# FNet and feed-forward on one core: sums of the second layer's moving side one by one among the remainders, other places for weights' sums

## The chip, the core and the metric

The kernel runs on one core of a Trainium2 chip. A core has a matrix engine, TensorE (PE), and three engines for elementwise work: VectorE (DVE), ScalarE (ACT) and GpSimd (POOL). SyncE (SP) issues most of the DMA transfers. The metric is device time of one launch in microseconds (us). The kernel before takes 688.23 us, the median of 3 runs (687.84 to 688.51). The profile is of one further execution of 686.36 us.

## The reference

One sequence of 2048 rows with 512 columns, and a feed-forward layer of 1792 columns, all in fp32:

```python
a = jnp.einsum("bsd,ed->bse", x, dft_hid_re)
b = jnp.einsum("bsd,ed->bse", x, dft_hid_im)
y = jnp.einsum("ts,bse->bte", dft_seq_re, a) - jnp.einsum("ts,bse->bte", dft_seq_im, b)
...
h = x + A_ref(layernorm(x), dft_seq_re, dft_seq_im, dft_hid_re, dft_hid_im)
h2 = h + B_ref(layernorm(h), w1, w2)     # B_ref(x) = silu(x @ w1) @ w2
```

## The kernel before, in words

**Three matmuls for one.** PE multiplies in fp32r, which holds fewer bits than fp32. Each fp32 operand is split into a rounded part (hi) and a remainder (lo). ACT writes the rounded part (L147) and DVE subtracts it from the source to get the remainder (L151). A product is then three matmuls, hi by hi, hi by lo, lo by hi (L196 to L198). In the names, `ph`, `gth` are rounded parts and `pl`, `gtl` their remainders. A remainder waits for its rounding, and a matmul that reads it waits for the remainder.

**Seven products for eight.** The sequence transform and both feed-forward layers use a scheme with seven products of blocks in place of eight. It needs sums and differences of the blocks ahead of the products, on both sides, and sums of the products behind them. For the second layer's moving side (the activations `g`) these are four subtractions for each pair `p` of blocks, in the function `sums_g` (L900). They are done in place: the first two make the operands of products 5 and 7, the last two those of products 6 and 4. Products 1, 2 and 3 read the blocks as they are or rounded before.

**The stages on the core.** `plain(0,0)` to 94 us, `fast(1,0)` to 168, `mix(0)` to 213, `fast(0,1)` and `fast(1,1)` to 367, `mix(1)` to 411: the transform along the sequence, and along the columns. Then the feed-forward layer: `up(0)` to 482 us, `down(0)` with its first products (1, 2 and 3) to about 507 and the others (6, 7, 5 and 4) to 546, `up(1)` to 614, `down(1)` likewise to 680. `norm_h(q, tau)` normalises the rows of half `q` between them: a mean (`m`), centring (`hr`), a square, a variance (`v`), a root, a scaling and a store to `nd`. Its two sums over all partitions are done by POOL (L624).

**What sets the order.** The program is a list of events, each with a planned time. `at(t, f)` puts one at a time, and `step(n, f, before, after)` puts `n` matmuls at the running clock of PE, with other events that stand a given number of microseconds ahead or behind. The sorted list sets the order of instructions on each of PE, DVE, ACT and POOL. Nothing overtakes on these engines: an instruction that waits holds those behind it. Planned times are only a means to sort; the instructions run as soon as what they wait for is done. SP's transfers are in program order too, and a load into a page waits for the page's last readers.

**Places.** There are 51 pages in SBUF, given out by a planner that follows the same planned times, so another time for an event also gives other pages to what comes after. PSUM has 4 tiles of 2 banks. `bank[n]` collects product `n` of the second layer over all seven pairs. When the last pair is done, ACT copies the bank to a page, `keep_bank(n)` (L918, `p` in the names), and the bank's place is used by another product. DVE's adds at L914 then put the kept products together into `r`.

**Numbers named below.** `LEADS` and the times in the loop over `sums_x` set when sums, roundings and remainders of `plain` and `fast` stand ahead of their products. `NORM_US` has the planned starts of `norm_h`, counted from the end of `mix(q)`. `sums_w1` and `make_w2` prepare the weights.

Of the kernel before, what the change touches and what calls it, by code (L numbers as in the profile page):

```python
# [12 lines left out]
ALU = mybir.AluOpType  # L13
# [16 lines left out]
WARM = 13  # L30
MM_US = 0.2265
PREP_US = 8.0
LEADS = (((0, 16.5, 6, 5), (1, 11, 6, 1), 10.5, 8.5),
         ((0, 21, 9, 6), (1, 16, 9, 7), 15, 13))
LOAD_US = 18.0
FETCH_US = 13.0
NORM_US = (-2, 62), (5, 6)
GAP_US = 2.2
FREE_US = {None: 2.0, "matmul": 4.0, "dma_start": 10.0}
ORDERED = (mybir.EngineType.PE, mybir.EngineType.DVE, mybir.EngineType.Activation, mybir.EngineType.Pool)  # L40

# [87 lines left out]
def program(nc, page, keep, small, psum, dram, x, xT, seq, hid, ffn, out):  # L129
# [27 lines left out]
    def halves(lead, make):  # L157

        kept = []
        return [(lead + GAP_US, lambda: kept.append(make())), (lead, lambda: kept.pop()())]  # L160

# [38 lines left out]
    events, clock = [], [0.0]  # L200
# [11 lines left out]
    def at(t, f):  # L212
        events.append((t, 1, len(events), f))
# [41 lines left out]
    def norm_x(jj, which, factors, direct=False, done=False):  # L255

        for k in sorted({k for k, _ in which}):
            if (jj, k) not in xc:
                xc[jj, k] = page(f"xc{jj}{k}")
            for i in range(2):  # L260
                if (i, k, jj) not in X:
                    X[i, k, jj] = page(f"X{i}{k}{jj}", F32R, (2, 2, 256))

        def put(o, k, a, e):
            bias, scale = factors[k, a]
            nc.scalar.activation(o, xraw[jj, k][:, a, e], AF.Identity, bias=bias, scale=scale)

        todo = []
        for k, a in which if direct else ():
            for i in range(0 if done else 2):  # L270
                put(X[i, k, jj][:, 0, a], k, a, slice(i * 256, (i + 1) * 256))
            put(xc[jj, k][:, a, :], k, a, slice(0, 512))
            todo += [(X[i, k, jj][:, 1, a], xc[jj, k][:, a, i * 256 : (i + 1) * 256], X[i, k, jj][:, 0, a]) for i in range(2)]
        if not direct:
            for k, a in which:
                put(xc[jj, k][:, a, :], k, a, slice(0, 512))
        for k in sorted({k for k, _ in which}):
            tiles = [a for kk, a in which if kk == k]
            b = slice(tiles[0], tiles[-1] + 1)
            if tiles[-1] == 1:  # L280
                xraw.pop((jj, k))
            for i in range(0 if direct else 2):
                t, src = X[i, k, jj], xc[jj, k][:, b, i * 256 : (i + 1) * 256]
                nc.scalar.activation(t[:, 0, b], src, AF.Copy)
                todo.append((t[:, 1, b], src, t[:, 0, b]))
        return todo

    def rest(todo):
        for o, a, b in todo:
            nc.vector.tensor_tensor(o, a, b, op=ALU.subtract)  # L290
# [13 lines left out]
    def round_s(jj, sums):  # L304
        todo = []
        for n, v in enumerate(sums):
            t = X["S", n + 1, jj] = page(f"S{n + 1}{jj}", F32R, (2, 2, 256))
            nc.scalar.activation(t[:, 0], v, AF.Copy)
            todo.append((t[:, 1], v, t[:, 0]))
        return todo  # L310

    late = {}

    def early(key, f):
        late[key] = f()
# [60 lines left out]
    def plain(c, q):  # L376
# [47 lines left out]
        for a in range(2):  # L424
            step(24, lambda a=a: [mul(0, 0, tau, [a], part[key]) for tau, key in enumerate(keys)])
        at(-98.5, lambda: load_x(0, 1))
        at(2.4, lambda: early("x0", lambda: norm_x(0, [(1, 0), (1, 1)], late.pop("r0")(), True)))
        at(6.4, lambda: rest(late.pop("x0")))
        for jj, k, tau in [(jj, k, tau) for jj in range(NJ) for k in range(2) for tau in range(2)][2:]:
            key = ("A", c, q, jj, k, tau)  # L430
            before = [(LOAD_US, lambda jj=jj, k=k, tau=tau, key=key: load_seq(c, q, jj, k, tau, key)),
# [1 line left out]
            after = []  # L433
# [17 lines left out]
                after.append((0, evac))  # L451
                after += [(4, lambda i=i, tau=tau: store_c(q, i, tau)) for i in range(2)]
            step(24, lambda jj=jj, k=k, tau=tau, key=key: mul(jj, k, tau, (0, 1), part.pop(key)), before, after)
        for jj, t in enumerate((32, 54, 76, 81)):
            at(t, lambda jj=jj: early(("s", jj), lambda: sums_x(jj)))
            at(t + 3, lambda jj=jj: early(("s", jj), lambda: round_s(jj, late["s", jj])))
            at(t + 6, lambda jj=jj: rest(late.pop(("s", jj))))

    def fast(c, q):

# [411 lines left out]
    def down(q, later):  # L872
# [17 lines left out]
        def round_two(p, f, names):  # L890
            (hi, lo), remainder = rounded(g[q, f], "gt")
            for tau, n in enumerate(names):
                mov[n, p] = hi[:, tau, :], lo[:, tau, :]
            return remainder

        def sums_g(p):
            a, b = g[q, 2 * p], g[q, 2 * p + 1]
            b11, b12, b21, b22 = a[:, 0, :], a[:, 1, :], b[:, 0, :], b[:, 1, :]
            for x, y, z in ((b11, b12, b11), (b12, b22, b12), (b22, b22, b11), (b21, b21, b22)):
                nc.vector.tensor_tensor(x, y, z, op=ALU.subtract)  # L900

        def mul(n, p, ms=(0, 1)):
            if p == 0 and 0 in ms:
# [12 lines left out]
        def keep_bank(n):  # L916
            kept[n] = page(f"p{n}")
            nc.scalar.activation(kept[n], bank[n], AF.Copy)  # L918
# [43 lines left out]
        for p, ns in [(0, (1, 2)), (1, (1, 2)), (0, (3,)), (1, (3,))] + [(p, ns) for p in range(2, NP) for ns in ((1, 2), (3,))]:  # L962
            before, after = [], []
            if ns == (1, 2):
                before = [(FETCH_US, lambda p=p: fetch_w2(p, U, 0)), *halves(PREP_US + 1, lambda p=p: round_one(p)),
                          *halves(PREP_US, lambda p=p: round_two(p, 2 * p + 1, (2, 3)))]
                if p == NP - 2 and not later:
                    before += [(LOAD_US, lambda k=k: load_r(*k)) for k in ((0, 0), (0, 1))]
            if p == NP - 1:
                after = [(0, lambda n=n: keep_bank(n)) for n in ns]  # L970
            step(6 * len(ns), lambda p=p, ns=ns: [mul(n, p) for n in ns], before, after)
            if (p, ns) == (0, (1, 2)):
                yield
        if not later:
            for n, f in enumerate((lambda: add(kept[2], kept[2], kept[1]), lambda: add(r[0, 0], r[0, 0], kept[2]),
                                   lambda: store(0, 0), lambda: add(r[0, 1], r[0, 1], kept[3]))):
                at(clock[0] + 19 + n, f)
        first = clock[0] - PREP_US - 9
        for p in range(NP):
            t = first + 5 * p  # L980
            at(t - 2 * GAP_US - 1, lambda p=p: sums_g(p))
            for d, f in (*halves(1, lambda p=p: round_two(p, 2 * p, (5, 7))),
                         *halves(0, lambda p=p: round_two(p, 2 * p + 1, (4, 6)))):
                at(t - d, f)
        whole, part4 = (0, 1), (0, 1) if later else (0,)
        order = [(n, p, part4 if n == 4 else whole) for p in range(4) for n in (6, 7, 5, 4)]
        order += [(n, p, part4 if n == 4 else whole) for n in (6, 7, 5, 4) for p in range(4, NP)]
# [12 lines left out]
            sums_later(clock[0] + 8)  # L1000

    plain(0, 0)
    for p, t in enumerate((16, -52, -35, 27, 79, 81, 13)):
        sums_w1(clock[0] + t, p)
    fast(1, 0)
    mix(0)
    fast(0, 1)
    fast(1, 1)
    mix(1)
    for p, t in enumerate((-341, -367, -21, -9, -31, 30, 43)):  # L1010
        make_w2(clock[0] + t, p)
    second = down(0, True), down(1, False)
    up(0, 57, lambda: next(second[0]))
    list(second[0])
    up(1, 24, lambda: next(second[1]))
    list(second[1])

    nc.vector.memset(warm, 0.0)
# [45 lines left out]
```

## Time and profile before

| | before |
|---|---|
| median of 3 runs | 688.23 us (687.84 to 688.51) |
| profiled execution | 686.36 us |
| its span | 684.4 us |
| granted clock of PE | 1.00 |
| PE busy | 676.9 us (99%), 2965 matmuls |
| DVE busy | 555.7 us (81%) |
| ACT busy | 338.8 us (50%) |
| POOL busy | 79.9 us (12%) |

The span is the part of the execution that the profiler sees, from the first instruction to the last. "L196 PE MATMUL f<-gth,wf" is a matmul of line 196 that reads `gth` and `wf` and writes `f`, and "<-ACT p L918" behind it says that the idle time before it ended when ACT had written `p` at line 918. In a timeline the first column is the start in us, the second the length of one or of several that follow each other (x3).

### The profile page before, as it was taken

Reading aid. Unit: us, or ns where it says so; the run is one execution under the profiler, and the core shown is the slowest. Engines: PE = TensorE matmul, PEld = TensorE weight load, DVE = VectorE, ACT = ScalarE, POOL = GpSimd, SP = SyncE. Lnnn points to the kernel's source line nnn. Section 1 sums busy time; section 2 is a strip of 40 time slices with the busy share of each in tenths; the row PEclk is TensorE's granted clock in tenths of the full one; section 3 lists DMA queues with packets and bytes.
Section 4 is the critical chain, followed back from the end, with each engine's and each line's share of the span. In section 5 each row is a group of like instructions: output and inputs, shape, how many; then the busy total and the mean of one; then the engine's idle time right before and its main releaser. Section 6 shows DMA issues by size and latency. Waiting matters only on the chain.

```text
span 684.4 us, 8367 instructions
## 1 busy us (share of the span) xinstructions
PE 676.9 (99%) x2965; PEld 554.7 (81%) x2965; DVE 555.7 (81%) x713; ACT 338.8 (50%) x422; POOL 79.9 (12%) x103
## 2 busy tenths in 40 slices
PE   8999999999999999999999999999999999999997
PEld 5888888888888888878888888888878888888785
DVE  6699997996938798996998998877999545549984
ACT  4754775444333443533453544657654444565510
POOL 1012110100103200230000115521000000000000
PEclk9999999999999999999999999999999999999999
DMA  8845889875387667567884699569996566466802
GB/s 319 326 152 233 275 315 369 299 263 185 129 305 276 212 187 278 205 246 278 303 340 162 227 415 332 177 240 339 418 368 230 200 273 239 181 249 252 296 37 92
DMA packets 57289, 174.90 MB, mean 256 GB/s; under 512 B 6432, under 2 KB 13856, under 8 KB 57248
## 3 DMA queue, kind: packets, MB, share of 16 engines
q1 hardware_dynamic: 46896, 138.56, 56.6%
q0 software_dynamic: 10208, 35.68, 13.7%
q8 instruction: 23, 0.38, 0.2%
q14 instruction: 18, 0.15, 0.1%
q10 hardware_dynamic: 144, 0.13, 0.1%
HBM read 135.54 MB, written 38.81 MB: 255 GB/s over the span
## 4 chain that ended last, share of the span: by engine, by line
PE 45%; DVE 10%; issue 1%; ACT 0%; DVEq 0%; ACTq 0%
PE y L196 6%; PE y L198 6%; PE y L197 6%; DVE gtl L151 4%; PE f L196 3%; PE f L197 3%; PE f L198 3%; PE m L197 3%; PE m L198 3%; PE m L196 3%; DVE g L900 3%; PE vx L196 3%; PE vx L198 3%; PE vx L197 3%; DVE pl L151 1%
## 5 line engine op out<-in xcount | busy, mean ns | idle before, releaser
L147 ACT ACTIVATE ph<-raw 128x1024 fp32r<-128x1024 f32 x98 | 101.5, 1057 | 106.1 <-DVE raw L508 62.9
L151 DVE TENSOR_TENSOR pl<-raw,ph 128x1024 fp32r<-128x1024 f32 x98 | 124.3, 1281 | 18.1 <-ACT ph L147 18.0
L197 PE MATMUL m<-pl,S 128*128 128x512 f32 x192 | 74.9, 390 | 0.2 <-DVE pl L151 0.2
L198 PE MATMUL m<-ph,S 128*128 128x512 f32 x192 | 74.7, 389 | 0.0
L196 PE MATMUL m<-ph,S 128*128 128x512 f32 x192 | 74.7, 389 | 0.0
L783 DVE TENSOR_TENSOR g<-vx,g 128x512 f32<-128x512 f32 x42 | 28.9, 688 | 48.7 <-PE vx L198 19.9
L508 DVE TENSOR_TENSOR raw<-raw,raw 128x1024 f32<-128x1024 f32 x48 | 58.4, 1217 | 7.1 <-DMA raw<-in_seq 7.1
L196 PE MATMUL f<-gth,wf 128*128 128x512 f32 x161 | 63.0, 391 | 0.9 <-ACT p L918 0.8
L197 PE MATMUL f<-gtl,wf 128*128 128x512 f32 x161 | 62.7, 389 | 0.0
L198 PE MATMUL f<-gth,wf 128*128 128x512 f32 x161 | 62.7, 389 | 0.0
L147 ACT ACTIVATE gth<-g 128x1024 fp32r<-128x1024 f32 x42 | 43.8, 1056 | 35.4 <-DVE g L900 29.6
L196 PE MATMUL m<-ph,X 128*128 128x512 f32 x144 | 56.1, 390 | 0.0
L198 PE MATMUL m<-ph,X 128*128 128x512 f32 x144 | 56.0, 389 | 0.0
L197 PE MATMUL m<-pl,X 128*128 128x512 f32 x144 | 56.0, 389 | 0.0
L151 DVE TENSOR_TENSOR gtl<-g,gth 128x1024 fp32r<-128x1024 f32 x42 | 49.7, 1218 | 0.0
L197 PE MATMUL c<-pl,X 128*128 128x512 f32 x112 | 43.7, 390 | 0.0
L198 PE MATMUL c<-ph,X 128*128 128x512 f32 x112 | 43.6, 389 | 0.0
L196 PE MATMUL c<-ph,X 128*128 128x512 f32 x112 | 43.4, 389 | 0.0
L197 PEld LDWEIGHTS m<-pl,S 128*128 128x128 f32 x192 | 36.1, 188 | 8.6 <-DVE pl L151 1.0
L196 PEld LDWEIGHTS m<-ph,S 128*128 128x128 f32 x192 | 36.0, 188 | 7.5
L198 PEld LDWEIGHTS m<-ph,S 128*128 128x128 f32 x192 | 36.0, 188 | 7.4
L780 ACT ACTIVATE g<-y 128x512 f32<-128x512 f32 x42 | 24.9, 595 | 28.2 <-PE y L198 28.2
(250 smaller groups left out, 1476.0 us busy)
## 6 DMA issues: line engine op xcount, KB each, us to landing
raw<-in_seq SPq DMA_DIRECT2D x98, 512.0 KB, 5.5
wf<-wd SPq DMA_DIRECT2D x56, 512.0 KB, 5.6
sf<-sd SPq DMA_DIRECT2D x28, 512.0 KB, 5.9
w<-in_ffn SPq DMA_DIRECT2D x28, 256.0 KB, 4.7
hid<-in_hid SPq DMA_DIRECT2D x8, 512.0 KB, 4.5
c<-cd SPq DMA_DIRECT2D x8, 512.0 KB, 6.5
h<-in_xT SPq DMA_DIRECT2D x8, 512.0 KB, 6.7
hd<-h POOLq DMA_DIRECT2D x8, 512.0 KB, 5.8
```

Of the source, the lines that this page charges most:

```text
L147: nc.scalar.activation(hi, src, AF.Copy, scale=sign)
L151: nc.vector.tensor_tensor(lo, src, hi, op=ALU.subtract)
L196: nc.tensor.matmul(acc, wh, mh, start=first, stop=False, skip_group_check=on)
L197: nc.tensor.matmul(acc, wh, ml, start=False, stop=False, skip_group_check=on)
L198: nc.tensor.matmul(acc, wl, mh, start=False, stop=last, skip_group_check=on)
L508: nc.vector.tensor_tensor(o, a, b, op=ALU.subtract)
L780: nc.scalar.activation(g[q, f][:, tau, :], src, AF.Copy)
L783: nc.vector.tensor_tensor(g[q, f][:, tau, :], src, g[q, f][:, tau, :], op=ALU.add)
L900: nc.vector.tensor_tensor(x, y, z, op=ALU.subtract)
```

## The change

- `sums_g(p)` with its four subtractions in one event becomes `sum_g(p, n)`, one subtraction for product `n`. Each has a planned time of its own, and so have the roundings and the remainders. The start and the pitch of the pairs, and the times of the two roundings, come from `SUMS_US`, for each half.
- ACT's copies of the first products' banks, `keep_bank(n)`, get 0.5 us behind their products in the planned time in `down(0)` and still 0 in `down(1)`.
- `norm_h(0, 0)` is planned for 4 us behind `mix(0)` where it was 2 us ahead, `norm_h(0, 1)` for 84 us where it was 62, and `norm_h(1, 1)` for 4 us where it was 6.
- `LEADS`, the times of the sums of `plain`'s moving side (`sums_x`), and of a row's normalisation at the start, are other numbers.
- `sums_w1` and `make_w2` get other times, and so do the loads of the normalised rows for `up(0)` and `up(1)`.

```diff
-LEADS = (((0, 16.5, 6, 5), (1, 11, 6, 1), 10.5, 8.5),
-         ((0, 21, 9, 6), (1, 16, 9, 7), 15, 13))
+LEADS = (((0, 17, 7.5, 7), (1, 11, 3, 2.5), 10.5, 9),
+         ((0, 22.5, 10, 7), (1, 19.5, 9, 1), 15.5, 12))
-NORM_US = (-2, 62), (5, 6)
+NORM_US = (4, 84), (5, 4)
+SUMS_US = (20.9, 5.7, 2.5, 3.9), (19.4, 5.3, 2.8, 2.4)
+KEEP_US = 0.5, 0
...
-        at(2.4, lambda: early("x0", lambda: norm_x(0, [(1, 0), (1, 1)], late.pop("r0")(), True)))
-        at(6.4, lambda: rest(late.pop("x0")))
+        at(3.9, lambda: early("x0", lambda: norm_x(0, [(1, 0), (1, 1)], late.pop("r0")(), True)))
+        at(7.9, lambda: rest(late.pop("x0")))
...
-        for jj, t in enumerate((32, 54, 76, 81)):
+        for jj, t in enumerate((27, 62, 80, 76)):
             at(t, lambda jj=jj: early(("s", jj), lambda: sums_x(jj)))
-            at(t + 3, lambda jj=jj: early(("s", jj), lambda: round_s(jj, late["s", jj])))
-            at(t + 6, lambda jj=jj: rest(late.pop(("s", jj))))
+            at(t + 4.5, lambda jj=jj: early(("s", jj), lambda: round_s(jj, late["s", jj])))
+            at(t + 8, lambda jj=jj: rest(late.pop(("s", jj))))
...
-        def sums_g(p):
+        def sum_g(p, n):
             a, b = g[q, 2 * p], g[q, 2 * p + 1]
             b11, b12, b21, b22 = a[:, 0, :], a[:, 1, :], b[:, 0, :], b[:, 1, :]
-            for x, y, z in ((b11, b12, b11), (b12, b22, b12), (b22, b22, b11), (b21, b21, b22)):
-                nc.vector.tensor_tensor(x, y, z, op=ALU.subtract)
+            x, y, z = {5: (b11, b12, b11), 7: (b12, b22, b12), 6: (b22, b22, b11), 4: (b21, b21, b22)}[n]
+            nc.vector.tensor_tensor(x, y, z, op=ALU.subtract)
...
-                after = [(0, lambda n=n: keep_bank(n)) for n in ns]
+                after = [(KEEP_US[q], lambda n=n: keep_bank(n)) for n in ns]
...
-        first = clock[0] - PREP_US - 9
+        first, pitch, r57, r46 = SUMS_US[q]
         for p in range(NP):
-            t = first + 5 * p
-            at(t - 2 * GAP_US - 1, lambda p=p: sums_g(p))
-            for d, f in (*halves(1, lambda p=p: round_two(p, 2 * p, (5, 7))),
-                         *halves(0, lambda p=p: round_two(p, 2 * p + 1, (4, 6)))):
-                at(t - d, f)
+            t = clock[0] - first + pitch * p
+            wait = {}
+
+            def parts(n, f, names, p=p, wait=wait):
+                wait[n] = round_two(p, f, names)
+
+            for d, f in ((0, lambda p=p: sum_g(p, 5)), (1.6, lambda p=p: sum_g(p, 7)), (3.2, lambda p=p: sum_g(p, 6)),
+                         (pitch + 0.8, lambda p=p: sum_g(p, 4)),
+                         (r57, lambda p=p, parts=parts: parts(5, 2 * p, (5, 7))),
+                         (pitch + r46, lambda p=p, parts=parts: parts(4, 2 * p + 1, (4, 6))),
+                         (pitch + 2.4, lambda wait=wait: wait[5]()), (pitch + 4, lambda wait=wait: wait[4]())):
+                at(t + d, f)
...
-    for p, t in enumerate((16, -52, -35, 27, 79, 81, 13)):
+    for p, t in enumerate((42, -62, -21, 34, 93, 103, -54)):
         sums_w1(clock[0] + t, p)
...
-    for p, t in enumerate((-341, -367, -21, -9, -31, 30, 43)):
+    for p, t in enumerate((-328, -343, -19, -10, -27, 30, 43)):
         make_w2(clock[0] + t, p)
...
-    up(0, 57, lambda: next(second[0]))
+    up(0, 41, lambda: next(second[0]))
...
-    up(1, 24, lambda: next(second[1]))
+    up(1, 14, lambda: next(second[1]))
```

PE's instructions and their order are the same before and after, and so is the number of instructions on every engine. What moves stands on DVE, ACT, POOL and SP. In the rows below the number behind a name belongs to the buffer; the lines of the helpers are two higher after the change (L149 for L147, L153 for L151), and L902 takes the place of L900.

ACT in `down(0)`, around the copies of the first three banks (`p`). The blocks of `g` in the order before are the two of pair 1, of pair 2 (3568, 3569), of pair 3 (3653, 3654), of pair 4 (3741, 3742), the first of each for products 5 and 7, the second for 4 and 6. Before:

```order
L147 ACTIVATE gth<-g_3568 128x1024
L147 ACTIVATE gth<-g_3569 128x1024
L147 ACTIVATE gth<-g_3653 128x1024
L147 ACTIVATE gth<-g_3654 128x1024
L918 ACTIVATE p_4258<-f_3992 128x1024
L918 ACTIVATE p_4260<-f_3999 128x1024
L147 ACTIVATE gth<-g_3741 128x1024
L918 ACTIVATE p_4273<-f_4064 128x1024
```

After, with pair 1 as (3485, 3486), pair 2 as (3570, 3571), pair 3 as (3654, 3655), pair 4 as (3741, 3742):

```order
L149 ACTIVATE gth<-g_3570 128x1024
L149 ACTIVATE gth<-g_3486 128x1024
L149 ACTIVATE gth<-g_3654 128x1024
L920 ACTIVATE p_4243<-f_3994 128x1024
L920 ACTIVATE p_4245<-f_4001 128x1024
L149 ACTIVATE gth<-g_3571 128x1024
L920 ACTIVATE p_4259<-f_4064 128x1024
L149 ACTIVATE gth<-g_3741 128x1024
```

The rounding of pair 2's second block now stands behind two copies, that of pair 3's second block and of pair 4's first behind all three. The rounding of a pair's first block stands ahead of that of the second block of the pair before.

DVE at the end of `down(1)`'s sums. The last two pairs are (4902, 4903) and (4969, 4970). Before:

```order
L151 TENSOR_TENSOR gtl<-g_4835,gth 128x1024
L151 TENSOR_TENSOR gtl<-g_4902,gth 128x1024
L900 TENSOR_TENSOR g_4969<-g_4969 128x512
L900 TENSOR_TENSOR g_4969<-g_4970,g_4969 128x512
L900 TENSOR_TENSOR g_4970<-g_4970,g_4969 128x512
L900 TENSOR_TENSOR g_4970<-g_4970 128x512
L151 TENSOR_TENSOR gtl<-g_4903,gth 128x1024
L151 TENSOR_TENSOR gtl<-g_4969,gth 128x1024
L151 TENSOR_TENSOR gtl<-g_4970,gth 128x1024
L914 TENSOR_TENSOR p_5298<-p_5298,p_5296 128x1024
L914 TENSOR_TENSOR r_5078<-r_5078,p_5298 128x1024
```

After:

```order
L902 TENSOR_TENSOR g_4969<-g_4969 128x512
L902 TENSOR_TENSOR g_4903<-g_4903 128x512
L902 TENSOR_TENSOR g_4969<-g_4970,g_4969 128x512
L153 TENSOR_TENSOR gtl<-g_4902,gth 128x1024
L902 TENSOR_TENSOR g_4970<-g_4970,g_4969 128x512
L153 TENSOR_TENSOR gtl<-g_4903,gth 128x1024
L902 TENSOR_TENSOR g_4970<-g_4970 128x512
L916 TENSOR_TENSOR p_5279<-p_5279,p_5277 128x1024
L916 TENSOR_TENSOR r_5078<-r_5078,p_5279 128x1024
L153 TENSOR_TENSOR gtl<-g_4969,gth 128x1024
L153 TENSOR_TENSOR gtl<-g_4970,gth 128x1024
```

The four sums of a pair no longer follow each other, remainders of other pairs stand between them, and two adds of L914 (now L916) have moved ahead of the last two remainders.

DVE in `fast(1,1)`, where `norm_h(0, 1)` meets the remainders that the products around 300 us read. The buffers are 2399 for the remainder ahead of the reduction and 2417, 2438 for the two behind it. Before:

```order
L151 TENSOR_TENSOR pl<-raw_2399,ph 128x1024
L622 TENSOR_TENSOR v_2492<-sq_2443,sq_2467 128x1024
L623 TENSOR_TENSOR v_2492<-v_2492 128x512
L151 TENSOR_TENSOR pl<-raw_2417,ph 128x1024
L151 TENSOR_TENSOR pl<-raw_2438,ph 128x1024
```

After, where the same three remainders read 2395, 2413 and 2431, and the first reduction (`m`) stands where the second stood:

```order
L153 TENSOR_TENSOR pl<-raw_2395,ph 128x1024
L153 TENSOR_TENSOR pl<-raw_2413,ph 128x1024
L153 TENSOR_TENSOR pl<-raw_2431,ph 128x1024
L624 TENSOR_TENSOR m_2515<-h_1747,h_1749 128x1024
L625 TENSOR_TENSOR m_2515<-m_2515 128x512
L153 TENSOR_TENSOR pl<-raw_2453,ph 128x1024
```

The two remainders that stood behind the sums of `v` now stand ahead of those of `m`, and `v` comes some fourteen instructions later.

## The prediction

> **What bounds the kernel now.** I read the page first, then TensorE's waits, then the stretches around each wait, on the engine that ends it. The page:
>
> ```profile
> span 684.4 us, 8367 instructions
> ...
> PE 676.9 (99%) x2965; PEld 554.7 (81%) x2965; DVE 555.7 (81%) x713; ACT 338.8 (50%) x422; POOL 79.9 (12%) x103
> ...
> L196 PE MATMUL f<-gth,wf 128*128 128x512 f32 x161 | 63.0, 391 | 0.9 <-ACT p L918 0.8
> ```
>
> TensorE (PE) is busy for 99% of the span, and the change leaves its instructions and their order alone. So the time can change only by the places where PE waits. The waits view names one that belongs to the second layer: its banks `f`, held up by ACT's copies `p`.
>
> ```profile
> PE f L196 <- ACT p L918: 0.8, 2, 0.6
> ```
>
> That view counts idle time, and a matmul's modelled end hides part of a gap. I measure a wait by starts instead. Undisturbed matmuls start 0.23 us apart; the first one after a wait takes 0.50 and the next starts 0.33 to 0.34 after it, 0.11 more than usual. So a wait costs (gap - 0.23) + 0.11. PE's rows at the turn from the first products to the others, `down(0)` near 505 and `down(1)` near 641:
>
> ```profile
> 503.71 0.39 PE L198 MATMUL f<-b,wf 128*128 128x512 f32 x1
> ...
> 506.43 0.39 PE L198 MATMUL f<-gth,wf 128*128 128x512 f32 x1
> ...
> 507.79 0.39 PE L198 MATMUL f<-gth,wf 128*128 128x512 f32 x1
> 508.25 0.50 PE L196 MATMUL f<-gth,wf 128*128 128x512 f32 x1
> 508.58 0.40 PE L197 MATMUL f<-gtl,wf 128*128 128x512 f32 x1
> ...
> 510.89 0.39 PE L198 MATMUL f<-gth,wf 128*128 128x512 f32 x1
> 511.90 0.50 PE L196 MATMUL f<-gth,wf 128*128 128x512 f32 x1 [0.62 <-ACT p L918]
> 512.24 0.40 PE L197 MATMUL f<-gtl,wf 128*128 128x512 f32 x1
> ...
> 641.05 0.39 PE L198 MATMUL f<-gth,wf 128*128 128x512 f32 x1
> ...
> 645.13 0.39 PE L198 MATMUL f<-gth,wf 128*128 128x512 f32 x1
> 645.73 0.50 PE L196 MATMUL f<-gth,wf 128*128 128x512 f32 x1 [0.21 <-ACT p L918]
> ```
>
> Three waits: 508.25 - 507.79 = 0.46, cost 0.34; 511.90 - 510.89 = 1.01, cost 0.89; 645.73 - 645.13 = 0.60, cost 0.48. Together 1.71 us. Each is a bank that is used again and must first be copied out by ACT. ACT's rows tell why the copies are late:
>
> ```profile
> 504.82 1.07 ACT L147 ACTIVATE gth<-g 128x1024 fp32r<-128x1024 f32 x1 [3.66 <-DVE g L900]
> 506.22 1.06 ACT L147 ACTIVATE gth<-g 128x1024 fp32r<-128x1024 f32 x1 [0.34 <-DVE g L900]
> 507.19 1.92 ACT L918 ACTIVATE p<-f 128x1024 f32<-128x1024 f32 x2
> 509.88 1.06 ACT L147 ACTIVATE gth<-g 128x1024 fp32r<-128x1024 f32 x1 [0.77 <-DVE g L900]
> 510.85 1.00 ACT L918 ACTIVATE p<-f 128x1024 f32<-128x1024 f32 x1
> ...
> 643.71 1.06 ACT L147 ACTIVATE gth<-g 128x1024 fp32r<-128x1024 f32 x1 [0.65 <-DVE g L900]
> 644.67 1.01 ACT L918 ACTIVATE p<-f 128x1024 f32<-128x1024 f32 x1
> ```
>
> The bank of `p1` was full at 503.71 + 0.39 = 504.10, but two roundings `gth` stand ahead of its copy, and both wait for DVE's sums (L900). The copy begins at 507.19. `p3`'s bank was full at 506.82 and its copy begins at 510.85, behind another `gth` that waits for sums. In `down(1)` `p3`'s bank is full at 641.44 and copied from 644.67. ACT was idle ahead of each of these roundings, so it is the order that holds the copies up, not ACT's work.
>
> The next largest waits lie in the first layer. One comes from a slow remainder on DVE beside a POOL reduction:
>
> ```profile
> 300.81 5.53 DVE L151 TENSOR_TENSOR pl<-raw,ph 128x1024 fp32r<-128x1024 f32 x3
> ...
> 301.15 3.98 POOL L624 PARTITION_ALL_REDUCE v<-v  x1 [16.10 <-issue]
> ...
> 301.67 0.39 PE L196 MATMUL m<-ph,S 128*128 128x512 f32 x1
> 302.08 0.50 PE L197 MATMUL m<-pl,S 128*128 128x512 f32 x1
> ...
> 304.71 0.39 PE L196 MATMUL m<-ph,S 128*128 128x512 f32 x1
> 305.26 0.50 PE L197 MATMUL m<-pl,S 128*128 128x512 f32 x1 [0.17 <-DVE pl L151]
> ...
> 78.18 0.39 PE L196 MATMUL c<-ph,X 128*128 128x512 f32 x1
> 78.56 0.50 PE L197 MATMUL c<-pl,X 128*128 128x512 f32 x1
> ```
>
> Three remainders that follow one another take 5.53 us, where three of 1.22 with their small overlap take 3.49 (a row below shows three): some 2.05 us are lost while POOL runs until 305.13. The waits of the remainder's readers: 0.41 at 302.08, cost 0.29; 0.55 at 305.26, cost 0.43; and, elsewhere in `plain`, 0.38 at 78.56, cost 0.26.
>
> **The change part by part.** *Second layer, ACT.* The sums become single events, and each pair's rounding for products 5 and 7 starts ahead of the fourth sum of the pair before. Call a block by half, pair and number (`g031`: half 0, pair 3, second block). Before, ACT rounds `g030` and `g031` ahead of `p1`, and `g040` ahead of `p3`. In the new order of `down(0)` `g030` alone stands there ahead of `p1` and `p2`, `g021` between `p2` and `p3`, and `g040` and `g031` behind all three. `p1` can run from 504.1 to 505.1, `p2` follows its bank, full two products of 0.68 us later (505.46), to 506.5. Then `g021` to 507.4 and `p3` to 508.4. PE would like to reuse the banks at 508.02 (507.79 + 0.23) and, with the first wait gone, at 510.8. Both waits go with about 2.5 us to spare: -1.23. In `down(1)` a single rounding stands between `p2` and `p3`, then `g130`; by the same steps (`p2` done at 641.1, two roundings of 1.06 less their overlap) `p3` is copied from 642.9 to 643.9, and is wanted at 645.36: -0.48. What is late next: a rounding moved behind `p2` makes its remainder `gtl` and what follows it on DVE wait, about 2.8 us in `down(0)` and 4 us in `down(1)`.
>
> *Second layer, DVE.* The number of sums and their duration stay. They stand among remainders now, where neighbours that don't depend on each other overlap by 0.08 us. But every rounding for 5 and 7 now stands on ACT ahead of that for 4 and 6 of the pair before, so its `gtl` waits some 0.4 us per pair. I count DVE's pace as unchanged. In `down(1)` the adds for `p2` and `r00` (L914) also stand ahead of the last two `gtl`:
>
> ```profile
> 655.14 3.49 DVE L151 TENSOR_TENSOR gtl<-g,gth 128x1024 fp32r<-128x1024 f32 x3
> 658.55 1.22 DVE L914 TENSOR_TENSOR p<-p,p 128x1024 f32<-128x1024 f32 x1
> ...
> 663.77 0.39 PE L197 MATMUL f<-gtl,wf 128*128 128x512 f32 x1
> ```
>
> Before, the last `gtl` ended at 658.63. Now, from the `gtl` that waits for the rounding behind `p2` (642.1), DVE has 11 operations of 1.22 (nine `gtl`, two adds) and 13 sums of 0.69 to do: 22.4 us, less about 24 overlaps of 0.08: the last `gtl` ends near 662.6. PE wants it at 663.77 - 0.48 = 663.29. It fits by 0.7 us. I cost it at 0; bounds 0 and what a delay beyond 0.7 costs, below. In `down(0)` the closest first use of a new remainder leaves over 4 us by the same counting.
>
> *First layer, `norm_h(0, 1)`* starts 22 us later. Its two reductions on POOL no longer stand beside remainders that are wanted at once. DVE does the four remainders around 300 before the reduction, instead of behind the centring and the first reduction, and is some 3 to 5 us ahead of PE from there on: -0.72 (0.29 + 0.43). The stores of the normalised rows are later by a similar amount, to about 350, and SP, which loads them again and works in order, waits for them near 354 to 358; the loads behind it (`hid`, the next weights) were issued at 355 to 362 before, so they come at about the same time. Cost 0; 1 to 2 us if the stores are later than I count.
>
> *`plain`.* Sums and rounding of the moving side (LEADS and the times of `sums_x`) come earlier. The remainder that PE read at 78.56 is then ready some 8 us ahead: -0.26. At the start one remainder now stands ahead of a row's refinement on DVE:
>
> ```profile
> 16.31 0.16 DVE L190 TENSOR_TENSOR rs<-rs 128x2 f32<-128x2 f32 x1 [0.61 <-POOL rs L168]
> ...
> 16.98 1.23 DVE L151 TENSOR_TENSOR pl<-raw,ph 128x1024 fp32r<-128x1024 f32 x1
> ...
> 18.03 0.62 PE L394 MATMUL c<-ph,X 128*128 128x512 f32 x2
> ```
>
> The 0.61 us in which DVE waited for POOL now holds part of a 1.23 us remainder. The refinement ends about 0.46 us later, and so do ACT's rounded rows X. PE had 0.3 us in hand at 18.03, so I count a wait of 0.19 + 0.11 = +0.3; bounds 0 (POOL earlier) and 0.6 (no slack at all).
>
> *The weights' sums and w1's preparation* move by up to 67 us among work of DVE, POOL and DMA. They have no reader on PE for tens of microseconds. I cost them at 0; bounds -0.3 and +1, three waits of the size of 78.56's.
>
> **Sum.** -1.23 - 0.48 - 0.72 - 0.26 + 0.3 = -2.4 us. Against the profiled execution, 686.36 us for a span of 684.4, that is 684.0. The median shown is 1.87 above that execution, so the change would be 688.23 - 2.4 = 685.8, a gain of 0.35%. A measurement can tell about 0.2% (1.4 us) from no change.
>
> **The rivals.** *Only the second layer gains.* A reduction may slow other remainders where it now stands. The row above shows what one costs: 2.05 us of DVE. If the two of `norm_h(0, 1)` meet remainders as near to PE as before, the 0.72 stays: 688.23 - 1.7 = 686.5. For it: DVE has `tensor_tensor` work nearly everywhere. Against: DVE's lead there of 3 to 5 us is more than 2.05. The Trainium skill's page "SBUF — State Buffer", section "Who interferes with whom", has the rule: an instruction of DVE with two SBUF inputs and a GpSimd instruction that reads SBUF exclude each other, and the later one fully blocks. The row agrees (the remainder ends 0.08 us after POOL does). By that rule the block moves with the reduction and can't be scheduled away, only placed where nobody is near.
>
> *The waits come back as others.* A remainder, a page or a load of the rearranged ones is late in three or four places by what the present waits cost (0.3 to 0.9): +1.2 to +2.5, so 687.0 to 688.3, within 0.2% of before. For it: PE is at 99%, every list is shifted, and I have counted three places with under 1 us in hand. Against: no engine but PE is above 81%.
>
> *Slower: the end of `down(1)`.* If DVE's list there loses 1.06 us per pair, because a sum waits for a remainder that waits for a rounding that waits for the sum before, then over the five pairs behind the rounding at 642 the last `gtl` comes 5.3 us later, at 667.9, and PE, which reads the remainders in the same order, stands still for 5.3 - 0.7 = 4.6 us: 685.8 + 4.6 = 690.4. It decides from a delay of 0.7 + 2.4 = 3.1 us on. Against: ACT was idle ahead of each rounding, and the list gives a rounding one to two DVE operations ahead of its remainder.
>
> **How the numbers follow.** Forecast as summed 0.47 (685.8; its own range 685.2 to 686.5), only the second layer 0.18 (686.5), waits come back 0.21, slower 0.14. The first two are faster by more than 1.4 us: 0.65. The third is within: 0.21. Slower 0.14. The predicted time is the likeliest, 685.8. The low end takes the -0.3 for the weights and another 0.6 for the start and small waits that I haven't counted: 684.9. The high end reaches into the third case, 688.2, and leaves out the fourth and its edge, under 2 in 10.
>
> **What would show it.** Right: PE's starts 0.23 us apart at the places of 508.25, 511.90 and 645.73; ACT's `p` copies directly behind their banks; POOL's reduction of `v` near 320, with a remainder of some 3.3 us beside it and no PE wait. Wrong: a PE wait on `gtl` between 655 and 664, on `m` between 300 and 345, or on a load behind 354; or a gap at 18 of more than 0.6 us.

## The result and the profile after

The changed kernel took 683.75 us, the median of 4 runs (683.43 to 684.04), beside 688.04 us for the kernel before (687.79 to 688.51): ratio 0.9939, 95% interval 0.9924 to 0.9955. That is 4.3 us less, where 2.4 were forecast (688.2 to 685.8), and 1.2 us below the low end of the range. Repeated, it took 684.59 beside 687.85 (ratio 0.9950, interval 0.9938 to 0.9963) and 684.52 beside 688.07 (0.9951, 0.9934 to 0.9968), so 3.3 to 3.6 us less. The direction and most of the mechanisms held; the size did not: the first result lies below the range, and so do the repeats, by 0.3 to 0.4 us.

The page of the changed kernel, and TensorE's waits:

```profile
span 681.5 us, 8362 instructions
...
PE 675.6 (99%) x2965; PEld 555.4 (81%) x2965; DVE 556.3 (82%) x713; ACT 338.2 (50%) x422; POOL 80.8 (12%) x103
```

```profile
PE idle L1036 <- DVE lower L1028: 1.2, 1, 1.2
PE c L396 <- DVE X L372: 0.4, 1, 0.4
```

The waits of `f` for ACT's copies and of `m` for DVE's remainders are no longer listed. What the view still lists sits at the start. From profile to profile (686.36 to 683.43 us, spans 684.4 to 681.5) the gain is 2.9 us.

In `down(0)`, ACT now copies each bank as soon as it is full. ACT's rows of the changed kernel:

```profile
502.17 1.06 ACT L149 ACTIVATE gth<-g 128x1024 fp32r<-128x1024 f32 x1 [3.16 <-DVE g L902]
503.21 1.03 ACT L920 ACTIVATE p<-f 128x1024 f32<-128x1024 f32 x1
504.51 1.03 ACT L920 ACTIVATE p<-f 128x1024 f32<-128x1024 f32 x1 [0.27 <-PE f L200]
505.43 1.05 ACT L149 ACTIVATE gth<-g 128x1024 fp32r<-128x1024 f32 x1
506.37 1.02 ACT L920 ACTIVATE p<-f 128x1024 f32<-128x1024 f32 x1
```

`p2` waits for its bank only ("<-PE f"), and `p3` ends at 507.39, some 2.4 us before PE reaches the product that had waited for it at 511.90 (in this execution at 509.75). PE is 1.0 us earlier here than in the profile before, so the prediction's 508.4 for the end of `p3` is right.

The reductions of `norm_h(0, 1)` still slow DVE, at their new places. POOL and DVE of the changed kernel:

```profile
301.94 4.06 POOL L626 PARTITION_ALL_REDUCE m<-m  x1 [9.26 <-DMA raw<-in_seq]
...
317.42 3.98 POOL L626 PARTITION_ALL_REDUCE v<-v  x1 [10.47 <-issue]
```

```profile
301.69 5.53 DVE L153 TENSOR_TENSOR pl<-raw,ph 128x1024 fp32r<-128x1024 f32 x3
...
318.22 3.26 DVE L510 TENSOR_TENSOR raw<-raw,raw 128x1024 f32<-128x1024 f32 x1
```

Three remainders again take 5.53 us, and a sum of 1.21 us takes 3.26 and ends with the reduction (321.48 and 321.40). PE waits at neither place, because DVE is ahead there: a little earlier it is DVE that waits for PE.

```profile
288.11 1.22 DVE L537 TENSOR_TENSOR p<-m,p 128x1024 f32<-128x1024 f32 x1 [4.51 <-PE m L200]
```

The loss moved with the reduction and kept its size of 2.05 us. The Trainium skill's page "SBUF — State Buffer", section "Who interferes with whom", calls what the two share an exclusive lock. The trace agrees in part: a sum that was blocked up to the reduction's end at 321.40 would still have its own 1.21 us to do and would end near 322.6, not at 321.48. So the block is shorter than the reduction as recorded (POOL's spans are rough), and the prediction's "The row agrees" says more than its row shows.

The end of `down(1)`, the slower rival's place, on DVE and PE of the changed kernel:

```profile
655.58 1.22 DVE L916 TENSOR_TENSOR p<-p,p 128x1024 f32<-128x1024 f32 x1
656.83 1.23 DVE L916 TENSOR_TENSOR r<-r,p 128x1024 f32<-128x1024 f32 x1
657.97 2.35 DVE L153 TENSOR_TENSOR gtl<-g,gth 128x1024 fp32r<-128x1024 f32 x2
```

```profile
660.93 0.39 PE L199 MATMUL f<-gtl,wf 128*128 128x512 f32 x1
```

The last `gtl` ends at 660.32 and PE first reads it at 660.93: 0.6 us in hand, where 0.7 was worked out.

At 18 us the wait that the prediction put at +0.3 is there (0.39 between starts). One that the kernel before had near 20 has gone: there PE stood 0.37 between starts, to 19.98 (cost 0.25). Before, and after:

```profile
19.98 0.74 PE L398 MATMUL c<-ph,X 128*128 128x512 f32 x2
```

```profile
17.87 0.39 PE L200 MATMUL c<-ph,X 128*128 128x512 f32 x1
18.26 0.73 PE L396 MATMUL c<-ph,X 128*128 128x512 f32 x2
```

### The profile page after: what moved, and what is told of

It is laid out like the page before. It is cut to its first block, busy times and chain, and to the rows that moved or that the text cites. A ratio compares the mean times of both kernels' runs of the same rounds, so it can differ in the third digit from the quotient of the medians.

```text
span 681.5 us, 8362 instructions
## 1 busy us (share of the span) xinstructions
PE 675.6 (99%) x2965; PEld 555.4 (81%) x2965; DVE 556.3 (82%) x713; ACT 338.2 (50%) x422; POOL 80.8 (12%) x103
## 4 chain that ended last, share of the span: by engine, by line
PE 98%; DVE 1%; DMA 0%; issue 0%; DVEq 0%
PE m L198 11%; PE m L200 11%; PE m L199 11%; PE y L198 8%; PE y L200 8%; PE y L199 8%; PE f L199 6%; PE f L200 6%; PE f L198 6%; PE c L200 4%; PE c L199 4%; PE c L198 4%; PE vx L200 3%; PE vx L199 3%; PE vx L198 3%; PE c L396 1%
## 5 line engine op out<-in xcount | busy, mean ns | idle before, releaser
L149 ACT ACTIVATE ph<-raw 128x1024 fp32r<-128x1024 f32 x98 | 101.8, 1058 | 109.8 <-DVE raw L510 61.4
L153 DVE TENSOR_TENSOR pl<-raw,ph 128x1024 fp32r<-128x1024 f32 x98 | 124.6, 1281 | 13.1 <-ACT ph L149 12.8
L510 DVE TENSOR_TENSOR raw<-raw,raw 128x1024 f32<-128x1024 f32 x48 | 60.5, 1260 | 5.8 <-PE m L199 3.6
L149 ACT ACTIVATE gth<-g 128x1024 fp32r<-128x1024 f32 x42 | 43.2, 1053 | 35.4 <-DVE g L902 29.8
L153 DVE TENSOR_TENSOR gtl<-g,gth 128x1024 fp32r<-128x1024 f32 x42 | 50.9, 1218 | 8.9 <-ACT gth L149 8.9
```

What stands on the lines that cost most here:

```text
L149: nc.scalar.activation(hi, src, AF.Copy, scale=sign)
L153: nc.vector.tensor_tensor(lo, src, hi, op=ALU.subtract)
```

## The experiments

To place a gain I cut PE's list of 2965 matmuls at fixed numbers (counted from 0) and took the time between the starts of the two at a stretch's ends. The lists are the same in every kernel of the table, so a stretch grows only by waits. All numbers are of profiled executions. "Root" is the start of POOL's first root for a row's normalisation, "start" the stretch from number 13 to 100 (about 7 to 27 us), 1200 to 1500 holds the waits near 290, 302 and 305, and 2100 to the last the second layer from `down(0)` on.

| kernel | root | start | 1200 to 1500 | 2100 to last | 100 to last | span |
|---|---|---|---|---|---|---|
| before | 9.15 | 20.37 | 68.93 | 197.69 | 652.46 | 684.4 |
| before, second profile | 10.75 | 21.44 | 68.75 | 197.69 | 652.30 | 685.5 |
| before, third profile | 9.76 | 20.87 | 68.83 | 197.63 | 652.32 | 684.9 |
| sums alone | 10.66 | 21.45 | 69.63 | 196.49 | 651.99 | 685.1 |
| norm_h and leads alone | 10.71 | 21.43 | 68.00 | 196.87 | 650.67 | 683.8 |
| all but the sums | 11.20 | 22.32 | 68.00 | 196.90 | 650.61 | 684.3 |
| all but norm_h and leads | 10.91 | 21.81 | 68.84 | 196.47 | 651.04 | 684.4 |
| all but the start | 11.05 | 21.98 | 68.00 | 195.84 | 649.34 | 682.8 |
| all but up(1)'s lead | 10.50 | 21.49 | 68.00 | 196.27 | 651.37 | 684.4 |
| changed | 9.24 | 20.37 | 68.00 | 195.84 | 649.55 | 681.5 |
| changed, second profile | 9.89 | 20.91 | 68.00 | 195.84 | 649.60 | 682.0 |
| changed, third profile | 10.90 | 21.97 | 68.00 | 195.84 | 649.53 | 683.0 |

**The kernel before, again.** No edit.

> The kernel before, unchanged, to see what its ordinary executions hold that its first profile (686.36 us, span 684.4) did not, since its median was 688.04. Theory A (the median carries waits that come and go): the spans of the timed runs spread over 684.4 to 686.5 and a profile of about 688 us shows 1 to 2 us of further gaps between PE's starts, beside the ones at 78, 302, 305, 508, 512 and 645. Theory B (what lies around the span differs, not the span): every span is about 684.4 and the difference of 1.7 us lies outside it.

Measured: median 688.25 (11 runs, 687.40 to 689.35), spans 685.5 to 687.4; profiled 687.51. The spans differ, so theory A. POOL and PE at the start of this profile:

```profile
9.96 0.81 POOL L1023 TENSOR_TENSOR spare<-spare,power 128x1 f32<-128x1 f32 x1 [9.10 <-issue]
10.75 0.55 POOL L168 TENSOR_TENSOR rs<-rs,power 128x1 f32<-128x1 f32 x1
```

```profile
18.06 0.39 PE L198 MATMUL c<-ph,X 128*128 128x512 f32 x1
19.04 1.23 PE L394 MATMUL c<-ph,X 128*128 128x512 f32 x4 [0.59 <-ACT X L266]
```

POOL's first operation, which waits for nothing that the profile shows ("issue"), begins 1.4 us later than the 8.57 of the first profile, and PE waits for the rounded rows X, 0.98 between starts. The first profile, on which the prediction's sum was made, had caught an early start. This second one lies below its median too (687.51 beside 688.25), so it shows a part of what the median holds and not all of it.

**The second layer's sums alone.**

```diff
+SUMS_US = (20.9, 5.7, 2.5, 3.9), (19.4, 5.3, 2.8, 2.4)
+KEEP_US = 0.5, 0
...
-                after = [(0, lambda n=n: keep_bank(n)) for n in ns]
+                after = [(KEEP_US[q], lambda n=n: keep_bank(n)) for n in ns]
...
-            at(t - 2 * GAP_US - 1, lambda p=p: sums_g(p))
...
+            for d, f in ((0, lambda p=p: sum_g(p, 5)), (1.6, lambda p=p: sum_g(p, 7)), (3.2, lambda p=p: sum_g(p, 6)),
```

> Only the second layer's part: single sums, SUMS_US and KEEP_US; all other numbers as before. By the prediction's steps 1.71 us less than before (waits at 508.25, 511.90 and 645.73 gone, the others left): about 686.3 against 688.0, ratio 0.9975. If the further gain of the whole change (4.3 us measured, 2.4 forecast) sits in the second layer: 3 us or more less.

Measured: 686.68 (8 runs) beside 688.23, ratio 0.9980 (0.9969 to 0.9990), 1.55 less. The waits at 508, 512 and 645 are gone, but one of 0.70 between starts is new, near the end of `down(0)`:

```profile
533.04 0.39 PE L198 MATMUL f<-gth,wf 128*128 128x512 f32 x1
533.74 0.50 PE L199 MATMUL f<-gtl,wf 128*128 128x512 f32 x1 [0.31 <-DVE gtl L153]
```

So the stretch from 2100 fell by 1.20 only, not by 1.71: the new wait costs 0.6. In this execution a wait near 290 showed too, although all that stands ahead of it is as before:

```profile
291.61 0.39 PE L200 MATMUL m<-ph,X 128*128 128x512 f32 x1
292.57 0.47 PE L198 MATMUL m<-ph,X 128*128 128x512 f32 x1 [0.57 <-ACT sq L647]
```

```profile
260.90 1.23 DVE L510 TENSOR_TENSOR raw<-raw,raw 128x1024 f32<-128x1024 f32 x1 [3.51 <-DMA raw<-in_seq]
```

In the second profile of the kernel before, whose start was as late, the same sum began at 260.10 and PE did not wait near 291. Here a load landed 0.8 us later; DVE, whose list is the same up to 484 us, had nothing in hand and carried the delay to 291 without a pause. The wait that this makes was 0.11 us in the first profile and 0.81 here.

**All but the sums.** Against the changed kernel the second layer's sums, roundings and copies go back to their old places; LEADS, `sums_x`, the start, the weights, `norm_h` and the leads stay as in the change.

```diff
-SUMS_US = (20.9, 5.7, 2.5, 3.9), (19.4, 5.3, 2.8, 2.4)
-KEEP_US = 0.5, 0
...
+            at(t - 2 * GAP_US - 1, lambda p=p: sums_g(p))
```

> All of the change but the second layer's sums and copies: LEADS, sums_x, the start, weights, norm_h and the loads' leads. By the prediction's steps -0.72 - 0.26 + 0.3 = -0.7 us: about 687.3, ratio 0.999. If the further gain sits in the first layer or in the loads: 2.5 us or more less, 685.5 or below, and the waits of about 508, 512 and 645 still there.

Measured: 685.76 (5 runs) beside 688.23, ratio 0.9965 (0.9952 to 0.9977), 2.5 less where 0.7 was expected. The further gain is on this side. And the second layer got shorter without its sums: 196.90 for 197.69. The wait at 508 was gone and that at 512 down to 0.61 between starts; the one at 645 stayed.

**The changed kernel, again.** No edit.

> The changed kernel again, on the same chip and beside the same executions of the kernel before as the next three. In the repeat of the kernel before, POOL's first operation began at 9.96 us where the first profile had 8.57, and all that follows on DVE, ACT and PE came 1.28 us later, with waits of 0.98 and 0.49 between starts at 18 and 21. Theory A1 (the late start of POOL costs both kernels alike, and the first profile of the changed kernel had a lucky one): the median comes out near 688.2 - 2.9 = 685.3, with single executions at 683.4. Theory A2 (the change also takes that cost away): the median stays at 683.8, with POOL's first operation as late as in the repeats.

Measured: 684.59 (5 runs, 683.54 to 684.68) beside 687.85. The median lies between what A1 and A2 gave; the profile had a root at 9.89 and a start of 20.91, and nothing from 100 on had moved (649.60).

**Roots of the first rows on DVE**, in the kernel before and in the changed one.

```diff
-        refine = rsqrt(v, t, r)
+        if jj == 0:
+            nc.vector.tensor_scalar(t, v, -0.5, None, op0=ALU.mult)
+            guess(v, t, b, r)
+            refine = lambda: steps(v, t, b, r)
+        else:
+            refine = rsqrt(v, t, r)
```

> The kernel before, where the first two normalisation roots of the start are worked out on DVE as the very first one is (two further iterations), so that the first rows no longer wait for POOL's first operations. Theory A (the median of before carries POOL's late start): the waits at 18 and 21 shrink or go, all executions fall together, and the median comes down by 1 to 1.7 us to 686.5 to 687.2; at the least the spread between executions shrinks below 1 us. Theory B (they have another origin): median 688.2 and a spread of 2 us as before.

> The same edit in the changed kernel: first roots on DVE, not on POOL. A1: 1 to 1.5 us less than the changed kernel measured beside it. A2: no difference within 0.5 us.

Measured: 688.34 (11 runs, 687.87 to 689.63) beside 687.85, and 685.67 (8 runs) for the changed kernel, 1.1 more than without the edit. Both expectations failed, and neither theory is decided by these runs: DVE's additional iterations made their own waits (PE 0.80 between starts at 8.8 and 1.07 at 18.1, 2.07 in the changed kernel), as large as the ones that POOL had made. The spread of 1.8 us in the first of them says that POOL's start is not the only thing that varies.

**All but norm_h and the leads of the loads.**

```diff
-NORM_US = (4, 84), (5, 4)
+NORM_US = (-2, 62), (5, 6)
...
-    up(0, 41, lambda: next(second[0]))
+    up(0, 57, lambda: next(second[0]))
...
-    up(1, 14, lambda: next(second[1]))
+    up(1, 24, lambda: next(second[1]))
```

> The changed kernel with norm_h's starts and the leads of the loads as before (NORM_US, up's 57 and 24). By the prediction's steps the waits at 302 and 305 come back: +0.72, and what the prediction left out at 290.67 and 439.87 too, +0.1 to +0.9: 0.7 to 1.6 us more than the changed kernel measured beside it. If the places moved by the weights' sums already freed DVE there: less than 0.4 more.

Measured: 686.65 (11 runs) beside the changed kernel's 684.59, 2.1 more. Between the two profiled executions the start differs by 0.9 (21.81 for 20.91), which the edit does not touch; 1.44 lies behind it: the waits at 302 and 305 (68.84 for 68.00) and again the one near 533 (0.69 between starts).

**POOL later, on purpose.** The first power operation three times.

```diff
-    nc.gpsimd.tensor_tensor(spare[:, :1], spare[:, 1:], power[:, :1], op=ALU.pow)
+    for _ in range(3):
+        nc.gpsimd.tensor_tensor(spare[:, :1], spare[:, 1:], power[:, :1], op=ALU.pow)
```

> The changed kernel with POOL's first power operation done three times in place of once, two more of about 0.57 us ahead of the first row's root. If POOL's start sets the first rows (theory A): PE's waits from 12 to 20 grow by 0.9 to 1.1 us and the median by as much. If something else does (DVE's work, as the roots on DVE left a spread of 1.5 us): under 0.3 us more.

Measured: 685.02 (5 runs) beside 684.52 for the changed kernel. The edit did not do what it was meant for; POOL's rows show the additional operations behind the root, not ahead of it, so neither expectation was tried:

```profile
9.32 0.71 POOL L1033 TENSOR_TENSOR spare<-spare,power 128x1 f32<-128x1 f32 x1 [8.46 <-issue]
10.01 0.58 POOL L170 TENSOR_TENSOR rs<-rs,power 128x1 f32<-128x1 f32 x1
10.56 1.69 POOL L1033 TENSOR_TENSOR spare<-spare,power 128x1 f32<-128x1 f32 x2
```

The run serves as one more point: root 10.01, start 20.94.

**The start as before.**

```diff
-        at(3.9, lambda: early("x0", lambda: norm_x(0, [(1, 0), (1, 1)], late.pop("r0")(), True)))
-        at(7.9, lambda: rest(late.pop("x0")))
+        at(2.4, lambda: early("x0", lambda: norm_x(0, [(1, 0), (1, 1)], late.pop("r0")(), True)))
+        at(6.4, lambda: rest(late.pop("x0")))
```

> The changed kernel with the normalisation at the start as before (2.4 and 6.4 in place of 3.9 and 7.9). By the prediction's step its wait at 18 shrinks by 0.46 and the one at 20 (0.25) comes back: 0.0 to 0.3 us less than the changed kernel for the same start of POOL. If this edit is what made the changed kernel's start cheap: 0.5 us or more longer.

Measured: 684.34 (5 runs) beside 684.52. Its start of 21.98 for a root at 11.05 lies with the others (21.97 for 10.90 with the edit), and the small wait at 29.81 is gone (649.34 for 649.55). By these numbers the edit costs about 0.2.

**One more profile of each.**

> A further profile of the kernel before: where POOL's first operation begins (8.57 and 9.96 so far) and whether PE waits at 290 (0.11 and 0 so far, 0.8 and 0.4 in kernels with the same first layer). If the start is a matter of each execution: between 8.5 and 10.7, with 0.5 us of waits up to 22 where it is early and 1.5 where it is late.

> A further profile of the changed kernel: POOL's first operation at 8.66 and 9.09 so far. If each execution draws its start anew: anywhere from 8.5 to 10.7, and waits of 0.5 to 2.2 us up to 22; behind 100 us no more than 0.35 us of waits in all, as in both profiles so far.

Measured: before 687.68 (8 runs), profiled 686.77, root at 9.76, start 20.87; changed 684.52 (4 runs), profiled 684.85, root at 10.90, start 21.97. The changed kernel meets the late start too:

```profile
18.17 0.39 PE L200 MATMUL c<-ph,X 128*128 128x512 f32 x1
19.64 0.73 PE L396 MATMUL c<-ph,X 128*128 128x512 f32 x2 [1.08 <-ACT X L268]
```

So the start belongs to the execution and not to the change: over all profiles with the root on POOL, 9.15 to 11.20 us for the root goes with 20.37 to 22.32 for the start, about 1 us for 1 us, with the edit at the start or without it. DVE's rows tell that POOL is the cause and that not everything comes late together. The operation that gives POOL the root's operand ends at 8.74 in the changed kernel's first profile and at 8.57 in the third, earlier where POOL is later. Then DVE's refinement of the root, in the first and the third:

```profile
10.12 0.21 DVE L190 SCALAR_TENSOR_TENSOR rs<-rs 128x1 f32<-128x1 f32 x1
```

```profile
11.48 0.22 DVE L190 SCALAR_TENSOR_TENSOR rs<-rs 128x1 f32<-128x1 f32 x1 [1.46 <-POOL rs L170]
```

Behind the start, the kernel before had no wait at 290 this time, but two that it had not shown, 0.45 between starts at 321 and 0.34 at 336.

**Only up(1)'s lead as before**, in the changed kernel.

```diff
-    up(1, 14, lambda: next(second[1]))
+    up(1, 24, lambda: next(second[1]))
```

> The changed kernel with only up(1)'s lead as before (24 in place of 14), which sets when the sums and remainders T of up(1) stand among down(0)'s on DVE. If it was this lead that cleared the way for down(0)'s last remainder (the two kernels without the norm_h part had a wait of 0.7 between starts near 533): that wait returns, 0.57 us, and the time from PE's hundredth matmul on grows from 649.55 to 650.1; the stretch around 302 stays free. If norm_h's own places did it: no wait at 533 and 649.55.

Measured: 685.50 (5 runs, 684.27 to 686.44) beside 687.96. The wait near 533 returns (0.48 between starts, 0.37 us with its restart), 1200 to 1500 stays at 68.00, and a new wait for a load of weights shows at the first product of `down(0)`, which was not expected:

```profile
481.04 0.39 PE L199 MATMUL f<-b,wf 128*128 128x512 f32 x1
482.55 0.50 PE L200 MATMUL f<-b,wf 128*128 128x512 f32 x1 [1.12 <-DMA wf<-wd]
```

From 100 on it took 651.37 where the changed kernel takes 649.55; 1.39 of the 1.82 is the load. With `norm_h`'s new places alone the last remainder of `down(0)` is late again, by less than with the old ones (0.48 for 0.69): its way is not clear without the lead.

**norm_h and the leads alone**, in the kernel before.

```diff
-NORM_US = (-2, 62), (5, 6)
+NORM_US = (4, 84), (5, 4)
...
-    up(0, 57, lambda: next(second[0]))
+    up(0, 41, lambda: next(second[0]))
...
-    up(1, 24, lambda: next(second[1]))
+    up(1, 14, lambda: next(second[1]))
```

> The kernel before with norm_h's starts and the leads of up alone as in the change. If norm_h's place is what slows the stretch from PE's matmul 1200 to 1500 (68.75 to 68.93 in the kernel before, up to 69.63 in kernels with the same first layer, 68.00 in the changed one): 68.00 here, 508, 512 and 645 still waited for, and a median 0.8 to 1.4 us below the kernel before. If the other edits of the first layer are needed as well: above 68.3.

Measured: 685.66 (5 runs) beside 687.96, ratio 0.9965 (0.9952 to 0.9977), 2.3 less, more than the 0.8 to 1.4 expected. 1200 to 1500 is 68.00 with this edit alone. And from 2100 on it takes 196.87 for 197.69, with DVE's and ACT's lists of sums and copies still in the old order: the wait at 508 is gone, that at 512 is down to 0.60 between starts.

```profile
506.69 1.92 ACT L918 ACTIVATE p<-f 128x1024 f32<-128x1024 f32 x2
509.32 1.06 ACT L147 ACTIVATE gth<-g 128x1024 fp32r<-128x1024 f32 x1 [0.71 <-DVE g L900]
510.29 1.01 ACT L918 ACTIVATE p<-f 128x1024 f32<-128x1024 f32 x1
```

The copies still stand behind the roundings, but DVE's sums and so the whole sequence are half a microsecond earlier than before (507.19 and 510.85 there), while PE's list, by the table's stretches, stands 0.2 us later at its number 2100 (482.2 for 482.0). DVE's rows ahead of `down(0)` show where it got ahead. The kernel before:

```profile
472.86 0.69 DVE L783 TENSOR_TENSOR g<-vx,g 128x512 f32<-128x512 f32 x1 [2.45 <-PE vx L198]
```

With `norm_h` and the leads alone:

```profile
470.46 1.28 DVE L673 TENSOR_TENSOR hr<-hr,v 128x512 f32<-128x512 f32 x2
473.09 0.69 DVE L783 TENSOR_TENSOR g<-vx,g 128x512 f32<-128x512 f32 x1 [1.34 <-PE vx L198]
...
481.25 0.69 DVE L783 TENSOR_TENSOR g<-vx,g 128x512 f32<-128x512 f32 x1 [0.39 <-PE vx L198]
```

The eight scalings of `norm_h` (L673) all stood behind 474 in the kernel before. Two of them now fill time in which DVE waited for PE, so that DVE waits for PE once more at 481.25, where it was behind before. They stand early with `up(1)`'s old lead too (470.23 in the run above) and late with the old `NORM_US` and leads (475.87 on), so it isn't that lead that moves them; in the program `NORM_US` sets their time.

## Why the prediction was right and wrong

*The second layer's ACT order: right, the sum a little short.* The three waits were put at 1.71 us and are gone; from matmul 2100 on the kernel gained 1.85 (197.69 to 195.84). The difference is in gaps of 0.23 to 0.25 that follow the restart, which the prediction's 0.11 leaves out. What the prediction did not see is that two edits were each worth a part of it: `norm_h` with the leads alone brought 0.82, the sums alone 1.20 with a new wait in them, and together 1.85. "In `down(0)` the closest first use of a new remainder leaves over 4 us" held for the whole change only (4.3 us in its profile); with the sums alone the last remainder ended 0.06 us before its first reader, which had waited for it.

*DVE at the end of `down(1)`: right.* 0.6 us in hand for 0.7.

*`norm_h(0, 1)`: right in kind, too small.* It was priced at the two waits that one profile showed, 0.72. The stretch gained 0.75 to 0.93 against the three profiles of the kernel before, and 1.3 to 1.6 against executions whose load at 259 came later (69.33 with the roots on DVE, 69.63 with the sums alone, both with the same order here). The wait at 290 (0.11), which the prediction left out, was a piece of the same thing: from 260 to 340 DVE in the kernel before had nothing in hand, so each late load or reduction came out on PE, at 290, at 302 and 305, or at 321 and 336. The change put a lead there (DVE waits 4.51 us for PE at 288.11), and all of them went at once. The fear that SP's loads behind 354 would suffer did not come true.

*The start: the size about right, by luck.* "I count a wait of 0.19 + 0.11 = +0.3" is there at 18, but the prediction counted only that side. The wait at 19.98 (0.25) went with it, so that for about the same root of POOL the stretch is as long with the change as without (20.37 and 20.37). And a wait of 0.16 came at 29.81, which goes when the start is as before. Together that is 0.2, for other reasons than the ones given.

*`plain`: right.* The wait at 78.56 went, 0.27 for 0.26. `LEADS`, the times of `sums_x` and the weights' places were not tried singly.

*The step that failed is the last of the sum*: "The median shown is 1.87 above that execution, so the change would be 688.23 - 2.4". The 1.87 us was carried over as if it were the same in both kernels. It is waits inside the span, since time and span differ by 1.8 to 2.1 us in short and long executions alike: the first profile of the kernel before had an early POOL and a load in time, and its span of 684.4 is shorter than that of all 87 timed executions whose spans are known (684.5 to 687.8, median 686.0). The changed kernel has less of these waits. Its 13 timed executions have spans of 681.5 to 683.0, median 682.5, which are the spans of its profiles with the earliest and the latest root; so its start alone can account for all that it varies. In the kernel before it can't: the widest difference between the starts of two profiles with the root on POOL, 1.95 us, would make it 686.3 at most, and 32 of the 87 are longer.

The forecast of 2.4 and the first result's 4.3 then differ by three pieces. The sum was short by 0.45 against the profiles (2.85 between the spans; 2.7 to 2.9 from matmul 100 on). Another 0.4 to 0.7 us are waits of the kernel before that its three profiles don't hold, since the medians of the repeats differ by 3.3 to 3.6. That these are the waits at 290 to 340 is inferred: two kernels with the same order there showed them with 0.4 to 0.9 us more, and they go with `norm_h` and the leads. The last 0.7 to 1.0 us I take for luck: the four executions of the first result had early starts. The profiled one, with POOL's root at 9.24, is one of them, and its three fellows were within 0.7 us of it, while the nine of the repeats have a median span of 682.7. The other profiles with the new start had roots from 9.89 to 11.20. That the three were early is inferred, since they have no trace.

*The rivals.* "Only the second layer gains" and "the waits come back as others" did not happen for the whole change. The second of them did for parts of it: the sums without the leads, and the change with `up(1)`'s old lead, each brought a wait of a remainder or a load. The slower case did not happen.

Open is what the longer executions of the kernel before hold (up to 689.8 us): its three profiles are of 686.36, 686.77 and 687.51 us, and none of an execution at its median or above was taken.

## What to carry to other kernels

A sum of waits from one profile is as good as that execution was typical: where the profiled execution is well below the median, look for what varies (a first operation that starts late, a load that lands late) and price the stretches in which an engine off the bottleneck has nothing in hand, not only the waits that this one execution showed. Compare kernels by stretches of PE's list with the variable start cut off. And try the edits of a joint change singly before dividing the gain among them: here the sums alone made a wait that the other half removed, and the other half alone took away a wait that the sums were thought to be needed for.

## What the hardware showed that was not expected

POOL's first operation, ahead of which the profile shows nothing that it waits for, began anywhere from 8.57 to 10.62 us in fifteen profiles, and through a chain of one root, a normalisation and a rounding it moved PE's list by about as much as it was late itself: 1 us for 1 us between roots at 9.15 and 11.20. This is read from the rows of these profiles; the two edits that were to set it apart (the roots on DVE, more operations on POOL) did not do so. Why POOL begins when it does stays open.
